# Squared-ReLU MLP on one core: block 0 opened with six whole-array f-tiles in place of four, worked off by row tiles of x, all first loads on one queue

## Chip, core and metric

One core of a Trainium2 chip (trn2). The metric is the device time of one execution in microseconds, median of the runs. One execution was also taken by the hardware profiler; all views of the profile and the trace are of that one.

## What is computed

Reference, cut to what matters (all tensors bf16):

```
B, S, D, F = 1, 2048, 576, 4608
h   = einsum("bsd,df->bsf", x, w1) + b1
r   = where(h > 0, h, 0)
out = einsum("bsf,fd->bsd", r * r, w2) + b2
```

That is two matrix products with a squared ReLU between them. x is 2048 x 576, w1 576 x 4608, w2 4608 x 576.

## The kernel before

**Tiling.** The 2048 rows of x are four blocks of 512 (`NSB`, `SB`), each of four row tiles of 128 (`RT`). The 4608 hidden features are 36 f-tiles of 128 (`NFT`). The contraction over D = 576 is four chunks of 128 (`NC`, the chunks 0 to 3) and a rest of 64 (rows 512 to 575).

**Phase A** computes the transposed, activated hidden values `hT` for every block: one PSUM bank of 128 x 512 floats for each f-tile. `a_step(b, j)` (L216) does two f-tiles at once, a *pair*: one of them uses rows 0 to 63 of the array and the other rows 64 to 127, in nine slices of 64 each (L213). This needs w1 in a form that holds 64 rows of D for one f-tile in the lower half of the partitions and 64 rows for the other in the upper half (`w1h`, loaded by `load_w1`, L97 to L99). `pairs` (L81) says which f-tiles make a pair; `slot` is its inverse. `evac_h` (L195) empties a bank: ACT does ReLU with the bias b1 (L197), DVE squares it (L199).

**Phase B** multiplies `hT` with w2 (L315, L329), adds b2 and stores.

**Block 0** is different at its start, since nothing has been loaded yet. Its first `G` = 4 f-tiles use the whole array, 128 rows deep: `qn` holds their four chunks of w1 (`load_quad`, L94), `qr` the rest of 64 rows (`load_rest`, L103). x arrives as it lies in memory, one row tile at a time (`load_x`, L91), is transposed on TensorE against an identity (L182) into PSUM, and copied from PSUM to `xT[0]` by DVE (L175) or ACT (L173). `transpose_chunks(half, cs, engs)` (L177) does this for *two* row tiles (a half, 256 columns) and the listed chunks; chunk `NC` stands for the last 128 columns of D and also fills the rest's place (L187). `full_mm(half, c)` (L225, L228) then multiplies chunk `c` of the four f-tiles with 256 columns of x. So this stage is two halves of 256 columns, and within each the four chunks. At its end four half-array matmuls add the rest (L254), three DVE copies put xT[0] into the form that the pair steps need (L256 to L258), and the four banks are emptied (L260). Then pair steps 2 to 17 follow (L292).

**What sets the order.** The schedule is written by hand: each engine works in the order of the program, and waits are for semaphores. The program order of L232 to L250 is TensorE's order. The eight first loads (four row tiles of x, four chunks of w1) are issued ahead of the start barrier (L126 to L140), alternating between SP's queue (x0, w1k0, w1k2, x3) and ACT's queue (x1, w1k1, x2, w1k3), where w1k0 is chunk 0 of w1 for the first f-tiles. Behind them SP issues the two rests and then the pairs of `w1h` in the order of their use (L121); a load takes one of eight semaphores in turn and waits until the load that used it before has landed. PSUM has eight banks; one takes the result of the five warm-up matmuls (L169), `G` of them are the f-tiles of block 0, and the remaining ones take transposes in turn. Blocks 1 to 3 read x by transposing DMAs (L266), behind the pair loads on SP. The pairs 0 and 1, which hold the first four f-tiles, are loaded after those of block 1 (L270) and come last in blocks 1 to 3 (L298).

Of the kernel before, what the change touches and what calls it, by code (L numbers as in the profile page):

```python
# [11 lines left out]
BF16 = mybir.dt.bfloat16  # L12
# [5 lines left out]
def kernel(  # L18
# [9 lines left out]
    nc = tc.nc  # L28
    P = 128
    H = 64  # L30
    x2 = x.flatten_outer_dims()
    out2 = out.flatten_outer_dims()
    S, D = x2.shape
    F = w1.shape[1]
    FH = F // 2
    G = 4
    NFT = F // P
    NJ = NFT // 2
    NC = D // P
    NH = D // H  # L40
    DM = NC * P
    SB = 512
    NSB = S // SB
    RT = SB // P
    HALF = SB // 2
# [9 lines left out]
    psum = ctx.enter_context(tc.tile_pool(name="psum", bufs=8, space=PSUM))  # L55

    def bank(name):
        return psum.tile([P, SB], FP32, name=name, tag="bank")
# [8 lines left out]
    at = [0]  # L67

    def early(n):
        at[0] += n  # L70
        assert at[0] <= NFT * D
        return w2_sb[:, at[0] - n:at[0]]


    xT = [early(XW).rearrange("p (w s) -> p w s", s=SB) for b in range(NSB - 1)]
    xT3 = xpool.tile([P, NH, SB], BF16, name="xT3", tag="xT3")
    xT.append(xT3[:])
    xs = early(RT * D).rearrange("p (j c) -> p j c", c=D)
    qn = early(NC * 4 * P).rearrange("p (c f) -> p c f", c=NC)
    qr = early(2 * P)  # L80
    pairs = [(0, 2), (1, 3)] + [(f, f + G) for f in range(G, NFT) if (f // G) % 2]  # L81
    slot = {ft: (h, j) for j, pr in enumerate(pairs) for h, ft in enumerate(pr)}
    assert len(pairs) == NJ and len(slot) == NFT

# [6 lines left out]
    def load_x(eng, j):  # L91
        eng.dma_start(out=xs[:, j, :], in_=x_view[:, j, :])

    def load_quad(eng, c):  # L94
        eng.dma_start(out=qn[:, c, :], in_=w1[c * P:(c + 1) * P, 0:G * P])

    def load_w1(eng, h, j0, n, cs):  # L97
        f0 = pairs[j0][h] * P
        eng.dma_start(out=w1h[h * H:(h + 1) * H, cs, j0 * P:(j0 + n) * P], in_=w1_rows[:, cs, f0:f0 + n * P])  # L99
# [1 line left out]
    NWARM = 5  # L101

    def load_rest(eng, h):  # L103
        eng.dma_start(out=qr[h * H:(h + 1) * H, :], in_=w1[DM:D, 2 * h * P:2 * (h + 1) * P])

    b1T = const.tile([P, NFT], FP32, name="b1T")
    warm = const.tile([P, 1], FP32, name="warm")
    load_x(nc.sync, 0)
    load_x(nc.scalar, 1)
    load_quad(nc.sync, 0)  # L110
    load_quad(nc.scalar, 1)
    load_quad(nc.sync, 2)
    load_x(nc.scalar, 2)
    load_x(nc.sync, 3)
    load_quad(nc.scalar, 3)
    nc.scalar.activation(out=warm[:], in_=nc.const_aps.tensor(1.0, [P, 1], FP32), func=ACT.Relu)
    for h in range(2):
        load_rest(nc.sync, h)


    for j0, n in ((2, 1), (3, 1), (4, 1), (5, 1), (6, 1), (7, 1), (8, 2), (10, 2), (12, 2), (14, 4)):  # L121
        for h in range(2):
            load_w1(nc.sync, h, j0, n, slice(0, NH))


    def issue_at_barrier(nc):  # L126
        entry, body = nc.main_func.blocks[:2]
        for engine in (mybir.EngineType.SP, mybir.EngineType.Activation):
            mine = [i for i in body.instructions if i.engine == engine and not isinstance(i, mybir.InstNoOp)]
            n = 0  # L130
            while isinstance(mine[n], mybir.InstDMACopy) and not mine[n].has_wait():
                n += 1
            assert n >= 3
            at = next(k for k, i in enumerate(entry.instructions)
                      if i.engine == engine and isinstance(i, mybir.InstEventSemaphore))
            for k, i in enumerate(mine[:n]):
                body.instructions.remove(i)
                entry.instructions.insert(at + k, i)

    nc.at_finalize(issue_at_barrier)  # L140


# [17 lines left out]
    ident = const.tile([P, P], BF16, name="ident")  # L160
# [10 lines left out]
    def copy_psum(eng, dst, src):  # L171
        if eng is nc.scalar:
            nc.scalar.copy(out=dst, in_=src)  # L173
        else:
            nc.vector.tensor_copy(out=dst, in_=src)  # L175

    def transpose_chunks(half, cs, engs):  # L177
        tps = [psum.tile([P, HALF], BF16, name="tp", tag="bank") for c in cs]
        for i in range(2):
            for c, tp in zip(cs, tps):  # L180
                d0 = c * P if c < NC else D - P
                nc.tensor.transpose(tp[:, i * P:(i + 1) * P], xs[:, 2 * half + i, d0:d0 + P], ident[:])  # L182
        cols = slice(half * HALF, (half + 1) * HALF)
        for c, tp, eng in zip(cs, tps, engs):
            copy_psum(eng, xT[0][:, c if c < NC else 7, cols], tp[:])
            if c == NC:
                nc.vector.tensor_copy(out=xT[0][0:H, 8, cols], in_=tp[H:P, :])  # L187

    def hT_of(b, ft):
        if b < NSB - 1:  # L190
            return hT[b][:, ft, :].rearrange("p (j s) -> p j s", j=RT)
        h, j = slot[ft]
        return w1h[:, h * RT:(h + 1) * RT, j * P:(j + 1) * P]

    def evac_h(b, ft, bk):  # L195
        r = rpool.tile([P, SB], BF16, name="r", tag="r")
        nc.scalar.activation(out=r[:], in_=bk[:], func=ACT.Relu, bias=b1T[:, ft:ft + 1], scale=1.0)  # L197
        r3 = r[:].rearrange("p (j s) -> p j s", j=RT)
        nc.vector.tensor_tensor(out=hT_of(b, ft), in0=r3, in1=r3, op=ALU.mult)  # L199

    def place(hi, c):
        if hi:
            return c // 2 if c % 2 else (3 + c // 2 if c else 8)
        return 8 if c == 8 else (4 if c % 2 else 0) + c // 2
# [11 lines left out]
    def a_step(b, j):  # L216
        bk = [bank("ph") for _ in range(2)]
        a_part(b, j, bk, range(NH))
        for h in range(2):
            evac_h(b, pairs[j][h], bk[h])  # L220


    bk0 = [bank("ph") for _ in range(G)]

    def full_mm(half, c):  # L225
        cols = slice(half * HALF, (half + 1) * HALF)
        for q in range(4):
            nc.tensor.matmul(bk0[q][:, cols], lhsT=qn[:, c, q * P:(q + 1) * P], rhs=xT[0][:, c, cols],  # L228
                             start=(half == 0 and c == 0), stop=False, skip_group_check=True)

    V, A = nc.vector, nc.scalar
    transpose_chunks(0, (0,), (V,))  # L232
    transpose_chunks(0, (1,), (A,))
    transpose_chunks(0, (2,), (A,))
    transpose_chunks(0, (NC,), (V,))
    full_mm(0, 0)
    transpose_chunks(0, (3,), (A,))
    full_mm(0, 1)
    full_mm(0, 2)
    transpose_chunks(1, (0, 1), (V, A))  # L240
    full_mm(0, 3)
    transpose_chunks(1, (2, NC), (A, V))
    full_mm(1, 0)
    transpose_chunks(1, (3,), (V,))
    full_mm(1, 1)
    b1T_ps = psum.tile([P, P], BF16, name="b1T_ps", tag="bank")
    nc.tensor.transpose(b1T_ps[:], b1_rows[:], ident[:])  # L247
    nc.vector.tensor_copy(out=b1T[:], in_=b1T_ps[:, 0:NFT])
    full_mm(1, 2)
    full_mm(1, 3)  # L250
    for i in range(2):
        for h in range(2):
            rows = slice(h * H, (h + 1) * H)
            nc.tensor.matmul(bk0[2 * h + i][:], lhsT=qr[rows, i * P:(i + 1) * P], rhs=xT[0][rows, place(h, 8), :],  # L254
                             start=False, stop=True, skip_group_check=True)
    nc.vector.tensor_copy(out=xT[0][0:H, 4:7, :], in_=xT[0][H:P, 0:3, :])  # L256
    nc.vector.tensor_copy(out=xT[0][H:P, 4:7, :], in_=xT[0][0:H, 1:4, :])
    nc.vector.tensor_copy(out=xT[0][H:P, 8, :], in_=xT[0][0:H, 0, :])  # L258
    for q in range(G):
        evac_h(0, q, bk0[q])  # L260


    def load_xT(b):
# [3 lines left out]

    load_xT(1)
    for h in range(2):
        load_w1(nc.sync, h, 0, 2, slice(0, NH))  # L270
    for b in range(2, NSB):
        load_xT(b)
    w2_view = w2_dram.rearrange("(ft p) d -> p ft d", p=P)
# [2 lines left out]
    def load_w2(c, n=1):  # L276
        nc.sync.dma_start(out=w2_sb[:, c * W2CH * D:(c + n) * W2CH * D].rearrange("p (ft d) -> p ft d", d=D),
                          in_=w2_view[:, c * W2CH:(c + n) * W2CH, :])
# [9 lines left out]
    def finish_xT(b):  # L288
        nc.vector.tensor_copy(out=xT[b][0:H, 8, :], in_=xT[b][H:P, 7, :])
        nc.vector.tensor_copy(out=xT[b][H:P, 8, :], in_=xT[b][0:H, 0, :])  # L290

    for j in range(2, NJ):  # L292
        a_step(0, j)
        if j == NJ - 2:
            finish_xT(1)
    load_w2(0)
    for b in range(1, NSB):
        for j in (*range(2, NJ), 0, 1):  # L298
            a_step(b, j)
            if j == NJ // 2 and b + 1 < NSB:  # L300
                finish_xT(b + 1)
        if b == 1:
            load_w2(1)
        if b == 2:
            load_w2(2, 2)
# [5 lines left out]
    for pr in range(NSB // 2):  # L311
        pc = bank("pc")
        for ft in range(NFT):
            for h in range(2):
                nc.tensor.matmul(pc[h * H:(h + 1) * H, :], lhsT=w2(ft, DM, D), rhs=hT_of(2 * pr + h, ft),  # L315
                                 start=(ft == 0), stop=(ft == NFT - 1))
# [52 lines left out]
```

## Time and profile before

| | us |
|---|---|
| median of 3 runs | 290.08 |
| lowest, highest | 289.96, 290.81 |
| the profiled execution | 290.45 |
| its span, first to last instruction | 288.7 |

The span is divided over TensorE's matmuls (PE, 99% busy), their weight loads (PEld, 46%), DVE (28%) and ACT (33%). Phase A lasts until about 145 us, phase B from there on. The stage that the change concerns is short: the first matmul of a pair step starts at 9.62 us.

How to read it: PE, DVE, ACT, POOL and SP are the engines TensorE, VectorE, ScalarE, GpSimd and SyncE. A line of the timeline gives start and length in us, the engine, the line of the kernel, the operation, what it writes and reads, how many, and in brackets how long the engine had been idle and for what. The buffers `xs`, `xT`, `qn` and `qr` are parts of `w2_sb`, since w2 comes later, so their names don't appear: "w_sb<-tp" is a copy from a transpose's bank into xT, "tp<-ident,w_sb" a transpose, "ph<-w_sb" a full_mm.

### The profile page before, as it was taken

The numbers are of one execution on the slowest core, as the hardware profiler recorded it, in microseconds if no ns is written. First come the engines' busy times: TensorE is split into PE (matmuls) and PEld (weight loads), VectorE is DVE, ScalarE is ACT, GpSimd is POOL, SyncE is SP. The second block draws the span as 40 slices with busy tenths as digits, with TensorE's granted clock in tenths as the row PEclk, the third lists the DMA queues.
The fourth block names the chain that finished last, engine by engine and source line by source line (L and its number), as shares of the span: only waits on it lengthen the run. The fifth ranks groups of instructions, "written<-read, shape, count | busy, mean of one in ns | idle before, by whom it ended". The sixth has DMA issues, their size and how long they took to land.

```text
span 288.7 us, 4818 instructions
## 1 busy us (share of the span) xinstructions
PE 284.9 (99%) x2067; PEld 133.7 (46%) x2078; DVE 79.5 (28%) x196; ACT 95.6 (33%) x153; POOL 1.5 (1%) x8
## 2 busy tenths in 40 slices
PE   9999999999999999999999999999999999999996
PEld 5544444444444444444445444444444444444454
DVE  1644454444445444444420011111100111111111
ACT  3666666766666676666620000000000000000000
POOL 2000000000000000000000000000000000000000
PEclk9999999999999999999999999999999999999999
DMA  7999999910400004300000100000000000000000
GB/s 200 205 190 204 172 185 208 321 50 2 122 3 0 3 2 142 106 0 2 0 2 19 20 20 20 20 23 5 15 20 23 20 20 20 23 20 22 20 23 20
DMA packets 35381, 18.01 MB, mean 62 GB/s; under 512 B 21652, under 2 KB 35360, under 8 KB 35360
## 3 DMA queue, kind: packets, MB, share of 16 engines
q1 hardware_dynamic: 34752, 17.14, 26.4%
q10 hardware_dynamic: 576, 0.56, 0.6%
q8 instruction: 16, 0.26, 0.4%
q14 instruction: 5, 0.04, 0.0%
q0 software_dynamic: 32, 0.01, 0.0%
HBM read 11.94 MB, written 2.36 MB: 50 GB/s over the span
## 4 chain that ended last, share of the span: by engine, by line
PE 98%; DMA 1%; issue 0%; DVE 0%; ACTq 0%
PE ph L213 47%; PE po L329 43%; PE pc L315 5%; PE ph L228 2%; DMA w_sb<-in_x_dram 1%; PE tp L182 1%; PE ph L254 0%; DVE o_sb L331 0%; PE b1T_ps L247 0%; ACTq L353 0%
## 5 line engine op out<-in xcount | busy, mean ns | idle before, releaser
L197 ACT ACTIVATE r<-ph,b1T 128x512 bf16<-128x512 f32 x144 | 91.0, 685 | 48.4 <-PE ph L213 46.4
L213 PE MATMUL ph<-w_sb,w1h 64*128 64x512 bf16 x936 | 101.2, 376 | 0.0
L213 PEld LDWEIGHTS <-w1h 64*128 64x128 bf16 x1260 | 61.3, 94 | 74.6
L329 PE MATMUL po<-w_sb,hT 128*128 128x512 bf16 x423 | 92.9, 379 | 0.5
L329 PEld LDWEIGHTS <-hT 128*128 128x128 bf16 x432 | 42.2, 98 | 51.2 <-issue 0.4
L199 DVE TENSOR_TENSOR hT<-r 128x512 bf16<-128x512 bf16 x108 | 46.0, 426 | 54.7 <-ACT r L197 54.2
L331 DVE TENSOR_TENSOR o_sb<-po,b_bc 128x512 bf16<-128x512 f32 (+2 forms) x17 | 11.2, 660 | 116.7 <-PE po L329 109.7
L213 PE MATMUL ph<-xT,w1h 64*128 64x512 bf16 x324 | 35.1, 376 | 0.0
L329 PE MATMUL po<-w_sb,w1h 128*128 128x512 bf16 (+2 forms) x178 | 31.2, 336 | 0.1
L329 PEld LDWEIGHTS <-w1h 128*128 128x128 bf16 x180 | 16.2, 98 | 15.3
L199 DVE TENSOR_TENSOR w1h<-r 128x512 bf16<-128x512 bf16 x36 | 15.3, 426 | 19.6 <-ACT r L197 19.5
L315 PE MATMUL pc<-hT,w_sb 128*64 128x512 bf16 x108 | 15.7, 379 | 0.0
L315 PEld LDWEIGHTS <-w_sb 128*64 128x64 bf16 x144 | 8.1, 110 | 7.6 <-issue 0.4
L315 PE MATMUL pc<-w1h,w_sb 128*64 128x512 bf16 x36 | 7.9, 379 | 0.0
L317 ACT ACTIVATE oc<-pc,b2T 128x512 bf16<-128x512 f32 x2 | 1.4, 687 | 13.7 <-PE pc L315 13.7
L325 DVE COPY o_sb<-oc 128x64 bf16<-128x64 bf16 x16 | 2.8, 172 | 9.3 <-DMA oc<-oc 9.3
L228 PE MATMUL ph<-w_sb 128*128 128x256 bf16 x32 | 5.3, 313 | 0.0
L228 PEld LDWEIGHTS <-w_sb 128*128 128x128 bf16 x32 | 3.4, 115 | 0.6
L175 DVE COPY w_sb<-tp 128x256 bf16<-128x256 bf16 x5 | 1.5, 292 | 5.9 <-PE tp L182 5.9
L182 PE MATMUL tp<-ident,w_sb 128*128 128x128 bf16 x20 | 2.7, 264 | 0.1
L169 PE MATMUL wps<-one 128*128 128x512 bf16 x5 | 2.3, 628 | 0.4 <-DVE one L144 0.4
L182 PEld LDWEIGHTS <-w_sb 128*128 128x128 bf16 x20 | 1.9, 118 | 1.4 <-DMA w_sb<-in_x_dram 1.2
(27 smaller groups left out, 10.7 us busy)
## 6 DMA issues: line engine op xcount, KB each, us to landing
w_sb<-in_w_dram SPq DMA_DIRECT2D x2, 1728.0 KB, 8.7
w1h<-in_w_dram SPq DMA_DIRECT2D x8, 288.0 KB, 5.9
out_dram<-o_sb SPq DMA_DIRECT2D x15, 144.0 KB, 1.8
w1h<-in_w_dram SPq DMA_DIRECT2D x12, 144.0 KB, 3.7
w_sb<-in_w_dram SPq DMA_DIRECT2D x2, 864.0 KB, 7.2
w1h<-in_w_dram SPq DMA_DIRECT2D x2, 576.0 KB, 11.2
w_sb<-in_x_dram SPq DMA_DIRECT2D x2, 144.0 KB, 3.4
w_sb<-in_x_dram ACTq DMA_DIRECT2D x2, 144.0 KB, 3.5
```

The source lines that it names most:

```text
L169: nc.tensor.matmul(wps[:], lhsT=ones[:, 0:P], rhs=ones[:], start=(i == 0), stop=(i == NWARM - 1))
L175: nc.vector.tensor_copy(out=dst, in_=src)
L182: nc.tensor.transpose(tp[:, i * P:(i + 1) * P], xs[:, 2 * half + i, d0:d0 + P], ident[:])
L197: nc.scalar.activation(out=r[:], in_=bk[:], func=ACT.Relu, bias=b1T[:, ft:ft + 1], scale=1.0)
L199: nc.vector.tensor_tensor(out=hT_of(b, ft), in0=r3, in1=r3, op=ALU.mult)
L213: nc.tensor.matmul(bk[h][:], lhsT=w1h[rows, c, j * P:(j + 1) * P], rhs=xT[b][rows, place(h, c), :], start=(i == 0), stop=(i == NH - 1))
L228: nc.tensor.matmul(bk0[q][:, cols], lhsT=qn[:, c, q * P:(q + 1) * P], rhs=xT[0][:, c, cols], start=(half == 0 and c == 0), stop=False, ski ...
L315: nc.tensor.matmul(pc[h * H:(h + 1) * H, :], lhsT=w2(ft, DM, D), rhs=hT_of(2 * pr + h, ft), start=(ft == 0), stop=(ft == NFT - 1))
L317: nc.scalar.activation(out=oc[:, pr, :], in_=pc[:], func=ACT.Identity, bias=b2T[:], scale=1.0)
L325: nc.vector.tensor_copy(out=o_sb[:, DM:D], in_=o_tr[pr][:, jj, h * H:(h + 1) * H])
L329: nc.tensor.matmul(po[:, 0:e - a], lhsT=hT_of(b, ft)[:, jj, :], rhs=w2(ft, a, e), start=(ft == 0), stop=(ft == NFT - 1))
L331: nc.vector.tensor_tensor(out=o_sb[:, a:e], in0=po[:, 0:e - a], in1=b2_bc[:, a:e], op=ALU.add)
```

## The change

Block 0 begins with six whole-array f-tiles in place of four (`G` = 6, `GP` = 3 pairs). The pairs are numbered anew: pairs 0 to 2 hold f-tiles 0 to 5, pairs 3 to 17 the others, and block 0 has the pair steps 3 to 17. The eight first loads are all issued on SP, in the order x0, w1k0, x1, w1k1, x2, w1k2, x3, w1k3, and w1's chunks are 768 columns wide instead of 512. ACT issues no loads any more. Transposes are made for each row tile by itself, two chunks into one bank (`transpose_tile`), with one copy of 2 x 128 columns by DVE or ACT; a third transpose holds the last 128 columns of D, with two copies. `full_mm(j, n, c)` multiplies chunk `c` of the six f-tiles with the columns of `n` row tiles from `j` on, so 128, 256 or 512 columns. The banks are emptied in the order of the rests. The late load of w1h has three pairs in place of two.

```diff
-    G = 4
+    G = 6
+    GP = G // 2
...
-    pairs = [(0, 2), (1, 3)] + [(f, f + G) for f in range(G, NFT) if (f // G) % 2]
+    pairs = [(i, GP + i) for i in range(GP)] + [(G + i, G + NJ - GP + i) for i in range(NJ - GP)]
...
-    load_x(nc.sync, 0)
-    load_x(nc.scalar, 1)
-    load_quad(nc.sync, 0)
-    load_quad(nc.scalar, 1)
-    load_quad(nc.sync, 2)
-    load_x(nc.scalar, 2)
-    load_x(nc.sync, 3)
-    load_quad(nc.scalar, 3)
+    for j in range(RT):
+        load_x(nc.sync, j)
+        load_quad(nc.sync, j)
...
-    for j0, n in ((2, 1), (3, 1), (4, 1), (5, 1), (6, 1), (7, 1), (8, 2), (10, 2), (12, 2), (14, 4)):
+    for j0, n in ((3, 1), (4, 1), (5, 1), (6, 1), (7, 1), (8, 1), (9, 1), (10, 2), (12, 2), (14, 4)):
...
+    def transpose_tile(j, c, n, eng):
+        cols = slice(j * P, (j + 1) * P)
+        tp = psum.tile([P, n, P], BF16, name="tp", tag="bank")
+        for k in range(n):
+            d0 = (c + k) * P if c < NC else D - P
+            nc.tensor.transpose(tp[:, k, :], xs[:, j, d0:d0 + P], ident[:])
+        c0 = c if c < NC else 7
+        copy_psum(eng, xT[0][:, c0:c0 + n, cols], tp[:])
+        if c == NC:
+            copy_psum(eng, xT[0][0:H, 8, cols], tp[H:P, 0, :])
...
+    V, A = nc.vector, nc.scalar
+    transpose_tile(0, 0, 2, V)
+    transpose_tile(0, 2, 2, A)
+    transpose_tile(0, NC, 1, V)
     bk0 = [bank("ph") for _ in range(G)]
...
+    def full_mm(j, n, c):
+        cols = slice(j * P, (j + n) * P)
+        for q in range(G):
             nc.tensor.matmul(bk0[q][:, cols], lhsT=qn[:, c, q * P:(q + 1) * P], rhs=xT[0][:, c, cols],
+                             start=(j == 0 and c == 0), stop=False, skip_group_check=True)
...
+    full_mm(0, 1, 0)
+    transpose_tile(1, 0, 2, V)
+    transpose_tile(1, 2, 2, A)
+    full_mm(1, 1, 0)
+    full_mm(0, 2, 1)
+    transpose_tile(1, NC, 1, V)
+    transpose_tile(2, 0, 2, A)
+    full_mm(2, 1, 0)
+    transpose_tile(2, 2, 2, V)
+    full_mm(2, 1, 1)
+    full_mm(0, 2, 2)
+    transpose_tile(2, NC, 1, A)
+    transpose_tile(3, 0, 2, V)
+    full_mm(3, 1, 0)
+    transpose_tile(3, 2, 2, A)
+    full_mm(3, 1, 1)
+    transpose_tile(3, NC, 1, V)
+    full_mm(2, 2, 2)
     b1T_ps = psum.tile([P, P], BF16, name="b1T_ps", tag="bank")
     nc.tensor.transpose(b1T_ps[:], b1_rows[:], ident[:])
     nc.vector.tensor_copy(out=b1T[:], in_=b1T_ps[:, 0:NFT])
+    full_mm(0, RT, 3)
```

The lines that these replace are in the kernel above (L177 to L187, L223 to L250).

More of the change, by code (lines that the diff above doesn't have):

```diff
@@ L78 @@
     xs = early(RT * D).rearrange("p (j c) -> p j c", c=D)
-    qn = early(NC * 4 * P).rearrange("p (c f) -> p c f", c=NC)
-    qr = early(2 * P)
-    pairs = [(0, 2), (1, 3)] + [(f, f + G) for f in range(G, NFT) if (f // G) % 2]
+    qn = early(NC * G * P).rearrange("p (c f) -> p c f", c=NC)
+    qr = early(GP * P)
+    pairs = [(i, GP + i) for i in range(GP)] + [(G + i, G + NJ - GP + i) for i in range(NJ - GP)]
     slot = {ft: (h, j) for j, pr in enumerate(pairs) for h, ft in enumerate(pr)}
@@ L103, in load_rest @@
     def load_rest(eng, h):
-        eng.dma_start(out=qr[h * H:(h + 1) * H, :], in_=w1[DM:D, 2 * h * P:2 * (h + 1) * P])
+        eng.dma_start(out=qr[h * H:(h + 1) * H, :], in_=w1[DM:D, GP * h * P:GP * (h + 1) * P])
     b1T = const.tile([P, NFT], FP32, name="b1T")
     warm = const.tile([P, 1], FP32, name="warm")
-    load_x(nc.sync, 0)
-    load_x(nc.scalar, 1)
-    load_quad(nc.sync, 0)
-    load_quad(nc.scalar, 1)
-    load_quad(nc.sync, 2)
-    load_x(nc.scalar, 2)
-    load_x(nc.sync, 3)
-    load_quad(nc.scalar, 3)
+    for j in range(RT):
+        load_x(nc.sync, j)
+        load_quad(nc.sync, j)
     nc.scalar.activation(out=warm[:], in_=nc.const_aps.tensor(1.0, [P, 1], FP32), func=ACT.Relu)
@@ L127, in issue_at_barrier @@
         entry, body = nc.main_func.blocks[:2]
[L128 to L138, printed above, removed]
+        engine = mybir.EngineType.SP
+        mine = [i for i in body.instructions if i.engine == engine and not isinstance(i, mybir.InstNoOp)]
+        n = 0
+        while isinstance(mine[n], mybir.InstDMACopy) and not mine[n].has_wait():
+            n += 1
+        assert n >= 2 * RT
+        at = next(k for k, i in enumerate(entry.instructions)
+                  if i.engine == engine and isinstance(i, mybir.InstEventSemaphore))
+        for k, i in enumerate(mine[:n]):
+            body.instructions.remove(i)
+            entry.instructions.insert(at + k, i)
     nc.at_finalize(issue_at_barrier)
@@ L175, in copy_psum @@
             nc.vector.tensor_copy(out=dst, in_=src)
[L177 to L187, printed above, removed]
+    def transpose_tile(j, c, n, eng):
[8 more added lines that the diff above has]
+            copy_psum(eng, xT[0][0:H, 8, cols], tp[H:P, 0, :])
     def hT_of(b, ft):
@@ L220, in a_step @@
             evac_h(b, pairs[j][h], bk[h])
+    V, A = nc.vector, nc.scalar
+    transpose_tile(0, 0, 2, V)
+    transpose_tile(0, 2, 2, A)
+    transpose_tile(0, NC, 1, V)
     bk0 = [bank("ph") for _ in range(G)]
-    def full_mm(half, c):
-        cols = slice(half * HALF, (half + 1) * HALF)
-        for q in range(4):
+    def full_mm(j, n, c):
+        cols = slice(j * P, (j + n) * P)
+        for q in range(G):
             nc.tensor.matmul(bk0[q][:, cols], lhsT=qn[:, c, q * P:(q + 1) * P], rhs=xT[0][:, c, cols],
[L229 to L245, printed above, removed]
+                             start=(j == 0 and c == 0), stop=False, skip_group_check=True)
[17 more added lines that the diff above has]
+    full_mm(2, 2, 2)
     b1T_ps = psum.tile([P, P], BF16, name="b1T_ps", tag="bank")
@@ L248 @@
     nc.vector.tensor_copy(out=b1T[:], in_=b1T_ps[:, 0:NFT])
-    full_mm(1, 2)
-    full_mm(1, 3)
-    for i in range(2):
+    full_mm(0, RT, 3)
+    for i in range(GP):
         for h in range(2):
             rows = slice(h * H, (h + 1) * H)
-            nc.tensor.matmul(bk0[2 * h + i][:], lhsT=qr[rows, i * P:(i + 1) * P], rhs=xT[0][rows, place(h, 8), :],
+            nc.tensor.matmul(bk0[GP * h + i][:], lhsT=qr[rows, i * P:(i + 1) * P], rhs=xT[0][rows, place(h, 8), :],
                              start=False, stop=True, skip_group_check=True)
@@ L258 @@
     nc.vector.tensor_copy(out=xT[0][H:P, 8, :], in_=xT[0][0:H, 0, :])
-    for q in range(G):
-        evac_h(0, q, bk0[q])
+    for i in range(GP):
+        for h in range(2):
+            evac_h(0, GP * h + i, bk0[GP * h + i])
     def load_xT(b):
@@ L269 @@
     for h in range(2):
-        load_w1(nc.sync, h, 0, 2, slice(0, NH))
+        load_w1(nc.sync, h, 0, GP, slice(0, NH))
     for b in range(2, NSB):
@@ L290, in finish_xT @@
         nc.vector.tensor_copy(out=xT[b][H:P, 8, :], in_=xT[b][0:H, 0, :])
-    for j in range(2, NJ):
+    for j in range(GP, NJ):
         a_step(0, j)
@@ L297 @@
     for b in range(1, NSB):
-        for j in (*range(2, NJ), 0, 1):
+        for j in (*range(GP, NJ), *range(GP)):
             a_step(b, j)
```

## The prediction

> **What bounds the kernel now.** I read the head of the page first, for whom the span belongs to.
>
> ```profile
> span 288.7 us, 4818 instructions
> PE 284.9 (99%) x2067; PEld 133.7 (46%) x2078; DVE 79.5 (28%) x196; ACT 95.6 (33%) x153; POOL 1.5 (1%) x8
> ```
>
> TensorE is busy for 99% of the span, so the change can gain only where TensorE idles or streams slowly, and loses wherever it makes TensorE wait. Next, the chain of work that ended last, in order of time (start, length, what). The change touches only its first 10 us.
>
> ```profile
> 0.21 2.84 DMA w_sb<-in_x_dram
> 3.04 0.05 issue
> 3.09 0.93 PE tp L182 x7
> 4.02 0.85 PE ph L228 x4
> 4.87 0.21 PE tp L182 x2
> 5.09 1.36 PE ph L228 x8
> 6.45 0.22 PE tp L182 x4
> 6.67 0.44 PE ph L228 x4
> ...
> 9.78 50.29 PE ph L213 x465
> ```
>
> See two things. After x1 lands at 3.05 no link but TensorE remains: no copy and no transfer of w1 is ever waited for. And the same four 128x256 matmuls take 0.85 us (0.213 each) at 4.02 and 0.44 (0.110) at 6.67; in thin slices of the timeline the starts go from 0.21 apart to 0.11 apart at 5.95 us. The array runs at half rate until 5.95. Four transposes take 0.22 us then, 0.055 for each 128 columns.
>
> Third, the timeline of all engines (start, length, engine, and in brackets the idle time before), for what a handoff costs.
>
> ```profile
> 3.42 0.29 DVE L175 COPY w_sb<-tp 128x256 bf16<-128x256 bf16 x1 [3.10 <-PE tp L182]
> ...
> 6.28 0.39 PE L182 MATMUL tp<-ident,w_sb 128*128 128x128 bf16 x4
> 6.65 0.29 DVE L175 COPY w_sb<-tp 128x256 bf16<-128x256 bf16 x1 [1.99 <-PE tp L182]
> 6.70 0.37 ACT L173 COPY w_sb<-tp 128x256 bf16<-128x256 bf16 x1 [1.21 <-PE tp L182]
> ...
> 9.17 0.11 PEld L254 LDWEIGHTS <-w_sb 64*128 64x128 bf16 x4 [0.21 <-issue]
> ...
> 9.62 35.56 PE L213 MATMUL ph<-w_sb,w1h 64*128 64x512 bf16 x328
> ```
>
> The transposes at 6.28 start 0.055 apart. The ACT copy at 6.70 begins 0.26 us after the last of them started (6.45) and takes 0.37; the DVE copy at 6.65 begins 0.26 after the third (6.39) and takes 0.29. So from the start of a transpose to a usable copy it is 0.63 us by ACT and 0.55 by DVE. Cold, the DVE copy at 3.42 began 0.33 after its transpose (3.09). In the kernel before, eight or more matmuls stand between, and nobody waits.
>
> Last, the busy time by stretches (us, then PE, PEld, DVE, ACT, POOL, clock, DMA share, GB/s): two queues early, and one queue of 1152-byte rows late.
>
> ```profile
> 2.00:2.50 0.50, 0.50 (x2) 0.00 (x0) 0.00 (x0) 0.35 (x1) 0.42 (x1) 1.00 1.07 375
> ...
> 54.00:55.00 1.00, 1.00 (x14) 0.45 (x10) 0.27 (x1) 0.51 (x1) 0.00 (x0) 1.00 1.09 386
> ```
>
> One queue moves as much as two (386 against 375 GB/s).
>
> **What the Trainium skill says.** "TensorE: Matmul & The Clock Gate", section "What's actually happening": the array's clock is halved until one free-running window of about 3.4 us was busy. The trace agrees on the halving (0.213 against 0.110 us) and puts the release at 5.95; which share of a window must be busy it doesn't show. The same page, "Step-by-step: what each phase is for": weight loads may be pulled ahead, matmuls stay in program order; so one matmul that waits for a copy stops all behind it. Section "Back-to-back issue gap": a stream of load and matmul pairs with 128 columns is sustained at some 81 ns each; this trace shows 55 in bursts of four. "DMA: Bandwidth & Descriptors", section "Issuing engines are not separate DMA queues": all queues share the 16 engines, a second issuer saves only issue time; the two rates above agree.
>
> **The change part by part.** The two kernels are compared where six f-tiles of block 0 are streamed; from there on both run the same pair steps.
>
> Streaming: before, four f-tiles of 4x512 columns, 2x512 for the paired rests, and one pair step of 9x512: 13,824 columns. After, 6x4x512 + 3x512 = 13,824. Both have 20 transposes of x and one of b1. So nothing is saved in streaming. Before reaches this point at 9.62 + 1.94 (a pair step: 35.56/328 x 18 = 1.95; copies of successive pairs come 1.94 apart) = 11.56 us. Cutting 128x512 into 128 and 256 columns adds some 2.5 ns a matmul (0.110 against 0.107): under 0.1 us.
>
> Transfers: eight on SP, 0.44 us of issue each (SP's row for L92, L95: 0.39 to 0.43), so the last is issued at 3.6 instead of 2.0. In order they hold 147, 344, 492, 688, 836, 1032, 1180, 1376 KB in sum. Before, x0 landed at 2.69 and the first four transfers (557 KB) by 3.7. With the same ramp I put x0, w1k0, x1, w1k1, x2, w1k2, x3, w1k3 at 2.7, 3.2, 3.7, 4.2, 4.7, 5.4, 5.8, 6.4. TensorE asks for them, by the working below, at 2.7, 3.5, 4.3, 5.6, 6.5, 8.0, 8.7, 11.0. Even at 200 GB/s (the mean of 18 to 30 us) from 1.1 us on, and 0.4 for the landing, all but x0 would be there in time (w1k1, 688 KB: 4.9; w1k3, 1376 KB: 8.4); none costs anything. The rests and the pair loads queued behind on SP start at 4.9 instead of 4.3, but the first pair is wanted at 13, not at 9.6, and a pair (295 KB at 200 GB/s: 1.5 us) is used up in 1.94: cover 3 us or more. ACT loses four issues, and its table load (at 2.15 now) may come sooner; its first copy is not waited for.
>
> Start: TensorE needs x0 only, and no longer idles until x1 (2.82 to 3.09 less the fill, 0.25 us at half rate): a gain of 0.13 in full-rate time.
>
> New waits, in program order, with 0.05 us from the copy's end to the matmul (the trace shows no such wait; the other way round, PE to DVE or ACT, takes 0.03 to 0.04, so between 0.02 and 0.10):
> 1. Three groups of transposes, 2.71 to 3.24 (five at 0.107). The first copy: second transpose's start 2.82 + 0.33 + 0.29 + 0.05 = 3.49. TensorE waits 0.25 at half rate. Then six matmuls to 4.15.
> 2. Row tile 1: four transposes from 4.15 to 4.58; its first copy is ready at 4.26 + 0.33 + 0.29 + 0.05 = 4.93: wait 0.35, at half rate. Six matmuls to 5.6, and w1k1 (six of 256 columns, the clock rising in them) to 6.4.
> 3. Row tile 2: its copy is on ACT and full_mm(2,1,0) comes right after the transposes, with nothing between: 0.63 + 0.05 - 0.055 = 0.63 us, at full rate.
> 4. Row tile 3, on DVE, likewise: 0.55 + 0.05 - 0.055 = 0.55.
> 5. full_mm(2,2,2) needs the ACT copy of row tile 3, behind six matmuls and one transpose (0.39): 0.63 + 0.05 - 0.39 - 0.03 = 0.26.
> Full-rate waits: 0.63 + 0.55 + 0.26 = 1.44. The half-rate ones, 0.60, count half as long as the release stays at 5.95 (work not streamed before it is streamed after it in half the time): 0.30. Sum: 1.44 + 0.30 - 0.13 = +1.6 us. Walking the same working through the kernel before gives its first pair step at 9.42 against the 9.62 recorded; the 0.2 is the "issue" before the half-array weights, which both have.
>
> After that point: six banks are copied out by ACT (0.69 each) instead of four; two banks are free for the next step, and the third step needs two of the six 1.9 us after the first is done, when ACT has finished them (1.4). No wait. The copies of L256 to L258 (1.39 us on DVE) end before the step's sixth slice asks. x of block 1 landed at 36.5 and is wanted at 40.7. The rest is untouched.
>
> So +1.6 us on the profiled execution (290.45, its span 288.7 and 1.75 outside): 292.1. That one stood 0.37 above the median of the runs, so the forecast is 290.08 + 1.6 = 291.7.
>
> Bounds: handoffs -0.1 to +0.2; 128-column matmuls at 81 ns instead of 55, 24 of them warm: 0 to +0.6; x0 landing sooner without x1 beside it: -0.1 to 0; the release between 4 and 7 us: -0.7 to +0.5. Together 291.0 to 292.5.
>
> **The rivals.**
> Late clock. Waits 1 and 2 take 0.60 of the 3.4 us before 5.95, so that window is 82% busy, where it was 93%. If that isn't enough, the release comes a window later, at 9.36: 3.4 us more run at half rate (1.7 lost), and wait 3 then counts half (0.3 back): 1.6 + 1.7 - 0.3 = +3.0, so 293.1. For it: the window of the warm-up matmuls, some 63% busy, was not enough. Against: 82 is nearer to 93.
>
> Early clock, no slower. The window runs free. If the release falls at 2.5 to 3.0 us, right behind the warm-up matmuls, which now run into the transposes without the gap at 2.7, the 3.2 us from 2.71 to 5.95 stream at full rate (1.6 gained), and waits 1 and 2 count in full, some 0.85 with the quicker groups before them: 1.44 + 0.85 - 0.13 - 1.6 = +0.55, so 290.6, within 0.3%. A release before about 3.5 us is the point from which it decides. Against it: the trace of before shows 5.95 with the same warm-up.
>
> Transfers bind after all. If one queue brings the eight 1.06 us apart, twice the 0.53 of my times, w1k0 lands at 3.8, x1 at 4.8, w1k1 at 5.9, x2 at 6.9 and w1k3 at 10.1: TensorE then waits at half rate for w1k0 (0.5, in place of wait 1), x1 (0.4) and the copy behind it (0.4), and later for x2 (0.1): 0.65 + 0.1 + 1.44 - 0.13 = +2.1, so 292.2. The 386 GB/s on one queue speak against it.
>
> **How the numbers follow.** The forecast's case has 0.58, binding transfers 0.05, late clock 0.16, early clock 0.15, a gain for a reason that I don't see 0.06. 0.3% is 0.87 us, about what a measurement of this kernel can tell from no change: faster 0.06, same 0.15, slower 0.79. The range runs from the early clock with handoffs 0.1 shorter (290.5) to the late clock with handoffs 0.2 longer (293.3), which leaves out little more than the unseen gain.
>
> **What would show it.** In the profile after, waits of the full matmuls for DVE and ACT copies of about 0.3, 0.4, 0.6, 0.55 and 0.25 us before 11 us; none for a transfer but x0; the first pair step at about 13.2; the page from there as before. Wrong would be: a pair step by 12, matmuls waiting for w1, 128-column matmuls 80 ns apart, or 0.21 us for 256 columns still after 6.5.

## The result and the profile after

| | before, us | after, us |
|---|---|---|
| median (lowest to highest) | 290.02 (289.95 to 290.81), 4 runs | 292.02 (291.50 to 292.22), 4 runs |
| profiled execution | 290.45 | 291.50 |
| its span | 288.7 | 289.7 |
| first matmul of a pair step in it | 9.62 (step 2) | 12.62 (step 3) |

The ratio of after to before, of the means, is 1.0060, with a 95% interval of 1.0038 to 1.0082. The forecast was 291.7, from +1.6 us; the medians lie 2.0 us apart.

The head of the page after, to be held against the one of before:

```profile
span 289.7 us, 4844 instructions
PE 284.8 (98%) x2078; PEld 134.1 (46%) x2090; DVE 79.8 (28%) x199; ACT 95.5 (33%) x154; POOL 1.5 (1%) x8
```

TensorE's busy time, as the profile counts it, is the same to 0.1 us; the span is 1.0 us longer. What was added is idle time. The chain that ended last shows where, in order of time (start, length, what):

```profile
0.53 2.80 DMA w_sb<-in_w_dram
3.33 0.05 issue
3.38 0.82 PE ph L227 x6
4.20 0.23 PE tp L178 x2
4.43 0.02 issue
4.45 0.30 DVE w_sb L171
4.75 0.04 issue
4.79 1.24 PE ph L227 x12
6.03 0.18 PE tp L178 x3
6.21 0.02 issue
6.24 0.38 ACT w_sb L169
6.62 0.04 issue
...
8.46 0.30 DVE w_sb L171
8.76 0.04 issue
...
9.45 0.38 ACT w_sb L169
9.83 0.04 issue
```

Before, this chain stayed on TensorE from 3.09 us on. Now it leaves TensorE four times for a copy, DVE, ACT, DVE, ACT in turn, and once at the start for w1k0. Each time the pattern is the same: transposes, 0.02 us, a copy, 0.04 us, matmuls. The timeline gives the lengths:

```profile
3.99 0.63 PE L178 MATMUL tp<-ident,w_sb 128*128 128x128 bf16 x4
...
4.79 1.24 PE L227 MATMUL ph<-w_sb 128*128 128x128 bf16 x12 [0.17 <-DVE w_sb L171]
...
5.87 0.33 PE L178 MATMUL tp<-ident,w_sb 128*128 128x128 bf16 x3
...
6.66 0.49 PE L227 MATMUL ph<-w_sb 128*128 128x128 bf16 x6 [0.46 <-ACT w_sb L169]
...
8.09 0.33 PE L178 MATMUL tp<-ident,w_sb 128*128 128x128 bf16 x3
...
8.80 0.49 PE L227 MATMUL ph<-w_sb 128*128 128x128 bf16 x6 [0.38 <-DVE w_sb L171]
...
9.58 0.22 PE L178 MATMUL tp<-ident,w_sb 128*128 128x128 bf16 x1
...
9.87 0.81 PE L227 MATMUL ph<-w_sb 128*128 128x256 bf16 x6
```

The brackets show less than what is lost. They count from the end of the last transpose's record, which is 0.22 us long (0.31 at half rate), while transposes that follow closely start every 0.055 us (0.107 at half rate). Counted from the start of the last transpose plus that step, TensorE waits 0.37 us before 4.79, 0.62 before 6.66, 0.54 before 8.80 and 0.23 before 9.87: the last transposes start at 4.31, 5.98, 8.20 and 9.58.

One quantity ties all runs together. The time of the profiled execution minus the start of its first pair step is 290.45 - 9.62 = 280.83 us before and 291.50 - 12.62 = 278.88 after, 1.95 apart, which is the pair step that six f-tiles save. After that point both kernels take the same time. So all of the difference, 12.62 - (9.62 + 1.94) = 1.06 us in this pair of executions, lies ahead of the first pair step.

The forecast's +1.6 stood for two releases of the clock at the same moment. They were not: the trace's record of the granted full clock begins at 5.95 us before and at 4.50 after. By the forecast's own rule (half of the time that TensorE streams, so from 4.79 to 5.95) that is worth some 0.6 us. With the release at 5.95 the changed kernel would have had its first pair step at about 13.2 us, as forecast, and the difference would have been some 1.6 us; both are estimates.

### The profile page after: what moved, and what is told of

Read it like the earlier page. It is cut to its first block, busy times and chain, and to the rows that moved or that the text cites. A ratio compares the mean times of both kernels' runs of the same rounds, so it can differ in the third digit from the quotient of the medians.

```text
span 289.7 us, 4844 instructions
## 1 busy us (share of the span) xinstructions
PE 284.8 (98%) x2078; PEld 134.1 (46%) x2090; DVE 79.8 (28%) x199; ACT 95.5 (33%) x154; POOL 1.5 (1%) x8
## 4 chain that ended last, share of the span: by engine, by line
PE 97%; DMA 1%; issue 0%; DVE 0%; ACT 0%; SPq 0%
PE ph L208 46%; PE po L331 43%; PE pc L317 5%; PE ph L227 2%; DMA w_sb<-in_w_dram 1%; PE tp L178 0%; ACT w_sb L169 0%; PE ph L255 0%; DVE w_sb L171 0%; SPq L93 0%; DVE o_sb L333 0%; PE b1T_ps L249 0%; SPq L355 0%
## 5 line engine op out<-in xcount | busy, mean ns | idle before, releaser
L208 PE MATMUL ph<-w_sb,w1h 64*128 64x512 bf16 x918 | 99.2, 376 | 0.0
L208 PEld LDWEIGHTS <-w1h 64*128 64x128 bf16 x1242 | 60.4, 94 | 73.6
L227 PE MATMUL ph<-w_sb 128*128 128x128 bf16 (+2 forms) x59 | 6.7, 258 | 1.3 <-DVE w_sb L171 0.6
L227 PEld LDWEIGHTS <-w_sb 128*128 128x128 bf16 x60 | 4.7, 102 | 2.7 <-issue 1.6
L171 DVE COPY w_sb<-tp 128x256 bf16<-128x256 bf16 (+2 forms) x10 | 2.5, 251 | 7.5 <-PE tp L178 7.4
L169 ACT COPY w_sb<-tp 128x256 bf16<-128x256 bf16 (+2 forms) x6 | 2.0, 336 | 5.6 <-PE tp L178 5.6
```

Of the source, the lines that this page charges most:

```text
L208: nc.tensor.matmul(bk[h][:], lhsT=w1h[rows, c, j * P:(j + 1) * P], rhs=xT[b][rows, place(h, c), :], start=(i == 0), stop=(i == NH - 1))
```

## The experiments

The theory: TensorE, in program order, waits for copies that come right behind their transposes. The rivals: the single queue and its later transfers; six f-tiles as such; the release of the clock. For each run, "step" is the start of the first pair step in its profile.

**Covered order.** Only TensorE's work in block 0 is altered: its order, and two groups of 256 columns are split into four of 128, so that their halves can stand apart:

```diff
     full_mm(1, 1, 0)
-    full_mm(0, 2, 1)
-    transpose_tile(1, NC, 1, V)
+    full_mm(0, 1, 1)
     transpose_tile(2, 0, 2, A)
+    full_mm(1, 1, 1)
+    transpose_tile(1, NC, 1, V)
     full_mm(2, 1, 0)
     transpose_tile(2, 2, 2, V)
     full_mm(2, 1, 1)
-    full_mm(0, 2, 2)
     transpose_tile(2, NC, 1, A)
     transpose_tile(3, 0, 2, V)
-    full_mm(3, 1, 0)
+    full_mm(0, 2, 2)
+    full_mm(2, 1, 2)
     transpose_tile(3, 2, 2, A)
+    full_mm(3, 1, 0)
     full_mm(3, 1, 1)
     transpose_tile(3, NC, 1, V)
-    full_mm(2, 2, 2)
+    full_mm(3, 1, 2)
```

> The changed kernel with nothing but the order of TensorE's work in block 0 altered, so that matmuls on older row tiles stand between a transpose and the first matmul that reads its copy. Waiting for copies (the theory): the waits of 0.62, 0.5 and 0.2 us in row tiles 2 and 3 go, about 0.2 stays before row tile 2; 1.1 us faster than the changed kernel, so some 0.6 us above the kernel before. One queue, or six f-tiles as such: no change, +1.7 to +2.0 us. Clock release: it follows no order of the program, so runs spread as before by some 0.8 us, and the profile's first pair step moves by half of what its release moves.

Measured: 290.87 us median of 8 runs against 290.03, ratio 1.0028 (1.0017 to 1.0038). The step came at 11.83 us, 0.79 before the changed kernel's, though its clock was released at 5.07, 0.57 later. The changed kernel streamed for 0.28 us of these 0.57 (from 4.79 on); half of that added, the order alone is worth some 0.9 us, where 1.1 was expected. It does not take back the whole loss: the run stands 0.84 us above the kernel before. The timeline shows what is left:

```profile
3.88 0.63 PE L178 MATMUL tp<-ident,w_sb 128*128 128x128 bf16 x4
4.68 1.04 PE L227 MATMUL ph<-w_sb 128*128 128x128 bf16 x12 [0.17 <-DVE w_sb L171]
5.72 0.28 PE L178 MATMUL tp<-ident,w_sb 128*128 128x128 bf16 x2
...
6.18 0.22 PE L178 MATMUL tp<-ident,w_sb 128*128 128x128 bf16 x1
6.46 0.49 PE L227 MATMUL ph<-w_sb 128*128 128x128 bf16 x6
```

The wait before 4.68 was left in it, and one of 0.22 us before 6.46 too (6.46 - 6.18 - 0.055). The transposes at 5.72 now wait some 0.2 us for x2, which landed at 5.67.

**Two queues.** The changed kernel with w1's chunks on ACT's queue:

```diff
     for j in range(RT):
         load_x(nc.sync, j)
-        load_quad(nc.sync, j)
+        load_quad(nc.scalar, j)
```

> The changed kernel with the four loads of w1's chunks on ACT's queue, x staying on SP's. Waiting for copies: x0 lands some 0.4 us later because w1k0 runs beside it, w1k0 sooner; within 0.3 us of the changed kernel, so +1.5 to +2.0 us on the kernel before. One queue as the cause: back to within 0.5 us of the kernel before.

Measured: 291.33 us against 290.03, 1.0050 (1.0038 to 1.0062). Its interval overlaps the changed kernel's, and its profile has the same waits (6.41 for ACT, 8.55 for DVE). Two queues alone bring no gain that the runs can tell; the queue by itself is not where the time went.

**Four f-tiles.** The changed kernel with `G = 4` (and the pair loads of before, from pair 2 on):

> The changed kernel's order and single queue, but four whole-array f-tiles as before. Waiting for copies: the waits stay, four matmuls instead of six hide 0.1 us less before the last; +1.6 to +2.1 us on the kernel before. Six f-tiles (their matmuls of 128 columns, their larger loads) as the cause: back to within 0.5 us of the kernel before.

Measured: 291.40 us against 290.03, 1.0050 (1.0038 to 1.0062). The loss stays with four f-tiles. In its profile TensorE waits for ACT and DVE copies in the same places, and here the last wait is long enough to have a bracket too:

```profile
PE ph L227 <- ACT w_sb L169: 0.6, 2, 0.5
PE ph L227 <- DVE w_sb L171: 0.6, 2, 0.4
```

A line gives the engine and line that waited, for whom, us in total, times, longest. The brackets hold 1.2 us, for four waits.

**The kernel before, exposed.** Two queues and four f-tiles as before; only the order around the second half is altered, so that its matmuls come right behind their transposes:

```diff
-    transpose_chunks(1, (0, 1), (V, A))
     full_mm(0, 3)
-    transpose_chunks(1, (2, NC), (A, V))
+    transpose_chunks(1, (0, 1), (V, A))
     full_mm(1, 0)
-    transpose_chunks(1, (3,), (V,))
     full_mm(1, 1)
+    transpose_chunks(1, (2, NC), (A, V))
+    transpose_chunks(1, (3,), (V,))
```

> The kernel before, two queues and four f-tiles, with the matmuls of the second half moved so that they come right behind the transposes that they need. Waiting for copies: about 0.5 us for chunk 0, 0.1 for chunk 1, 0.45 for chunk 2 and 0.1 for the last, all at full rate: +1.1 us on the kernel before, with neither one queue nor six f-tiles. One queue or six f-tiles as the cause: no change.

Measured: 291.44 us against 290.03, 1.0049 (1.0037 to 1.0061), +1.4. The loss of the change can be made in the old kernel without any other part of the change. The size is not clean, though:

```profile
PE ph L228 <- DMA w_sb<-in_w_dram: 0.6, 1, 0.6
...
PE ph L228 <- DVE w_sb L175: 0.3, 1, 0.3
PE ph L228 <- ACT w_sb L173: 0.2, 1, 0.2
```

Moving full_mm(0, 3) ahead of four transposes made it wait 0.6 us for w1k3, which nobody had waited for. The two copies' waits, with the 0.17 us each that the brackets leave out (0.22 - 0.055), come to some 0.9.

**Covered order on two queues.** As the covered order, with w1 on ACT's queue, with w1k1's first matmuls behind the second row tile's transposes, and with half of chunk 3's matmuls moved up between the transposes of the last row tile. The order against that of the covered run, in part:

```diff
     transpose_tile(1, 2, 2, A)
-    full_mm(1, 1, 0)
     full_mm(0, 1, 1)
+    full_mm(1, 1, 0)
     transpose_tile(2, 0, 2, A)
     full_mm(1, 1, 1)
     transpose_tile(1, NC, 1, V)
+    full_mm(0, 2, 2)
     full_mm(2, 1, 0)
     transpose_tile(2, 2, 2, V)
     full_mm(2, 1, 1)
     transpose_tile(2, NC, 1, A)
     transpose_tile(3, 0, 2, V)
-    full_mm(0, 2, 2)
+    full_mm(0, 2, 3)
...
-    full_mm(0, RT, 3)
+    full_mm(2, 2, 3)
```

> Six f-tiles with the covered order of the run before and the loads of w1 on ACT's queue, so that w1k1 and x2 land sooner and the first matmuls of w1k1 can stand behind the second row tile's transposes. Waiting for copies: nothing but the first copy (0.25 at half rate) is left; +0.0 to +0.5 us on the kernel before. Six f-tiles as the cause of what the covered order left (0.8): still +0.8.

Measured: 290.37 us against 290.41, 0.9999 (0.9991 to 1.0007). All six f-tiles, all matmuls of 128 columns, the larger loads and the row-tile order of x are in it, and it is as fast as the kernel before, within some 0.3 us. So none of these costs more than that by itself. The order alone left 0.84 us, two queues alone left 1.3, and both together leave nothing that can be measured. How much of the 0.84 the second queue took back, and how much the further changes of order, no run separates.

**The kernel before on one queue.** Its eight first loads all on SP, in the same order (`nc.scalar` replaced by `nc.sync` in L109 to L115):

> The kernel before with its eight first loads on SP's queue in the same order x0 x1 w1k0 w1k1 w1k2 x2 x3 w1k3. Waiting for copies: nothing of the 1.7 us comes from the queue itself, x1 lands some 0.3 us later (at half rate 0.15) and w1k3 is needed at 6.5 and lands about then; 0.0 to +0.4 us. One queue as the cause: +0.8 us or more.

Measured: 290.88 us against 290.41, 1.0019 (1.0011 to 1.0026): +0.5, a little above what was expected. One queue is not free here, for a reason that the expectation didn't name (engine and line, for whom, us in total, times, longest):

```profile
PE tp L182 <- DMA w_sb<-in_x_dram: 0.8, 2, 0.6
PE ph L213 <- DMA w1h<-in_w_dram: 0.5, 1, 0.5
```

There x2 and x3, which stand sixth and seventh on one queue, come late for the second half; and SP, busy with issues until 3.8, starts the pair loads at 5.17 instead of 4.30, so that at 22.4 us a pair step waits for its w1. The changed kernel's pair loads start at 5.17 too, but its first pair step is 3 us later.

**Repeats.** Both kernels again, for the release of the clock:

> The changed kernel unaltered, beside the others on the same chip. Waiting for copies: +1.7 to +2.0 us on the kernel before. If the moment of the clock's release is the same in every run, its profile shows 4.50 us again; if it runs free, another, with the first pair step later or earlier than 12.62 by about half of the difference.

> The kernel before unaltered, for its profile alone. If the release runs free of the program, it falls elsewhere than at 5.95 us, the first pair step moves from 9.62 by about half of the difference (not below 9.1, where its copies begin to be waited for), and the time of the execution moves with it, by the same amount; if not, all three repeat.

The changed kernel: 291.62 us against 290.41, 1.0041 (1.0027 to 1.0054). Its profiled execution took 293.58. In the trace's record the clock was released at 9.64 us, the first pair step was at 14.69, and the rest took 293.58 - 14.69 = 278.89 us, as in the first pair of profiles. Five microseconds of later release cost 2.07. Half rate shows directly:

```profile
1.00 3.23 DMA w_sb<-in_x_dram
...
5.05 2.08 PE L227 MATMUL ph<-w_sb 128*128 128x128 bf16 x12 [0.17 <-DVE w_sb L171]
```

The same twelve matmuls took 1.24 us in the profile after. The first line is the load of x1 in the chain that ended last: it landed at 4.23, and TensorE stood still for it from 3.89 to 4.28. So in this execution a transfer was waited for, besides the copies. The kernel before: 290.23, step at 9.39. This trace has no record of its clock's release, but the transposes after 4.5 us start 0.057 apart, so it lay at about 4.4: 1.5 us earlier than in the first profile, for a gain of only 0.23. From there on it waits for transfers, which half rate had hidden: for w1k2, which landed at 5.3, and for x3, at 6.0. The two profiles whose releases lie closest, 4.50 after and about 4.4 before, put the cost of the change at 12.62 - 9.39 - 1.94 = 1.29 us.

**Four f-tiles covered**, and the six beside it, for a version that might beat both kernels. The former is the covered version on two queues with `G = 4`; the latter is that version unaltered.

> The covered order on two queues with four whole-array f-tiles instead of six, so that the first loads are 262 KB smaller and land sooner; a try for a version that beats both. Waiting for copies: like the covered version with six, -0.3 to +0.1 us on the kernel before (the start on x0 alone gains 0.1, shorter cover may cost as much). Six f-tiles as a cause of loss: clearly below the covered version with six, -0.5 us or more.

> The covered version with six f-tiles on two queues, beside the one with four on the same chip: within 0.3 us of the kernel before, as in its first run. Its profile shows another release of the clock than 3.42 us if that runs free.

Measured: four 290.37 us against 290.25, 1.0000 (0.9991 to 1.0009); six 290.30, 1.0007 (0.9996 to 1.0018). Neither beats the kernel before, and four against six makes no difference that can be measured. In six's profile the release came at 3.81 us, in the first profile of that kernel at 3.42.

## Why the prediction was right, point by point

The time, 291.7 against 292.02, and the sign were right, and so was the cause in the main: with the copies covered and two queues the loss goes, with two queues alone it stays, and in the exposed kernel, with neither one queue nor six f-tiles, a loss of this kind comes. That the forecast lies within 0.3 us is in part luck: by the medians the change cost 2.0 us in the first set of runs and 1.2 in the repeat.

*Streaming saves nothing.* Right: six f-tiles covered equal four covered and the kernel before. The matmuls of 128 columns start 0.055 us apart in the profile after (six in 0.49 us, of which 0.16 is the way through the array), so the 81 ns of the Trainium skill ("TensorE: Matmul & The Clock Gate", section "Back-to-back issue gap") don't hold here, for groups of six to twelve.

*The waits.* Predicted 0.25, 0.35, 0.63, 0.55, 0.26; measured, counted as above, 0.36, 0.37, 0.62, 0.54, 0.23. The handoff from a copy to the matmul was taken at 0.05 and is 0.04. The first wait was not for the copy, which was ready at 3.24, but for w1k0, which landed at 3.33.

*Transfers.* This step failed in size. Times of 2.7, 3.2, 3.7, 4.2, 4.7, 5.4, 5.8 and 6.4 were given; they landed at 2.3, 3.3, 3.8, 5.2, 5.6, 6.4, 6.9 and 7.5 (issue and time to landing of each). "One queue moves as much as two" was read from a stretch at 54 us with 1152-byte rows; at the start it didn't hold. The same stretch before and after (GB/s at the end of the line):

```profile
1.00:5.00 4.00, 3.89 (x19) 2.07 (x18) 0.88 (x3) 2.12 (x4) 1.10 (x3) 1.00 0.95 282
...
1.00:5.00 4.00, 3.68 (x23) 2.17 (x22) 1.03 (x4) 1.93 (x4) 1.10 (x3) 1.00 0.89 242
```

The forecast's times stand for 1229 KB from x0's landing to the last one in 3.7 us, 332 GB/s; the measured ones for the same bytes in 5.2 us, 236 GB/s. Whether a second queue saves only the time to issue, as the prediction has it, is not settled by this: the eighth load was issued at 3.37 us instead of 1.58, and no run tells this from the queue itself. "None costs anything" was nearly true all the same in this profile, because TensorE, waiting for copies, asked late: 0.1 us for w1k0, and under 0.1 for w1k1, which landed at 5.16. In the repeat x1 cost 0.39 us at half rate. In the first covered version, where TensorE asks sooner, x2 cost some 0.2 us, and in the two-queue one still 0.3 in its second profile.

*The start on x0 alone.* Right in kind, larger: x0 landed at 2.3 us, and the first transpose started at 2.49 instead of 2.71.

*The range.* The bounds given, 291.0 to 292.5, are narrower than their own terms added up (290.8 to 293.0), which the prediction doesn't explain; 292.02 lies in both.

*The clock.* The rule (work not streamed at half rate takes half the time later) held: 2.07 us for 5.14 us of release in the changed kernel, where half of a wait that falls into the slow time is given back. The step that it gave, about 13.2, was for a release at 5.95. What failed is the reference: "the trace of before shows 5.95 with the same warm-up" was taken as typical. Over the ten profiles that record it the release lay between 3.4 and 9.6 us, in no order with the edits. So a single pair of executions can differ by about a microsecond for this alone, and 1.06 in the profiles and 2.0 between the medians don't contradict each other. The size of the loss from the two sets of runs is 1.2 to 2.0 us.

*The rivals.* Late clock did happen, in 1 of 10 executions of the changed kernel (293.58; worked out as 293.1), and a run of 292.64 of a covered version may be another; it isn't the usual case. Its reading of the trace was off: it took the window before 5.95 as 93% busy, which allows for the idle time before x1 (2.82 to 3.09) and leaves out that before x0 (2.53 to 2.71). By the starts of the matmuls, transposes counted, that window was busy for 87%. The section "What's actually happening" of the Trainium skill's page "TensorE: Matmul & The Clock Gate" has windows of about 3.4 us. Counted back from each release, in all ten profiles, the windows that led to a release were busy for 79% (covered on two queues, release 3.42) to 87% (before, and the first profile after). The window from 2.82 to 6.23 in the late execution was busy for about 70% (idle from 3.02 to 3.29 and from 4.68 to 5.05 for copies, from 3.89 to 4.28 for x1) and led to none. So waits in the first microseconds can go with a lost window, and the wait for a transfer was here as long as the longest one for a copy; that the waits were the cause, and how often it happens, was not tried. Early clock was not met: the changed kernel's own profiles show releases at 4.50 and 9.64 us, and one before 3.5 us, the forecast's point of decision, was seen only in the covered version. The nearest is the changed kernel on two queues, released at 3.73, in 291.25 us. Transfers that bind: refuted as a main cause by the two-queue run, though not as a part of the loss, since one queue cost the kernel before 0.5 us.

## What to carry to other kernels

On an engine that works in program order, the time from a transpose's start to the use of its copy (0.60 us by DVE, 0.68 by ACT here) has to be filled with work whose operands are already there; cutting the work into finer tiles shortened that filling here, so the order must be reworked with the tile size. When a covered order is moved forward, the next thing that it meets is a transfer: check each operand's landing against the new time of use, as the exposed kernel's 0.6 us shows. And compare short stages by a mark inside the program, here the first pair step, since behind it all runs of the same number of f-tiles agreed to 0.04 us, but for the one on one queue that waited later.

## What the runs showed of the hardware that was not expected

- The release of TensorE's clock fell at 3.42, 3.65, 3.73, 3.81, 3.84, 4.50, 4.68, 5.07, 5.95 and 9.64 us in the profiles that record it, twice differently for the same kernel (4.50 and 9.64; 3.42 and 3.81). The full clock is recorded for 283.31 or 286.72 us in every one of them, 3.41 apart, which fits windows of that length.
- At the start of the program, from 1 to 5 us, the five profiles with the first loads on one queue show 218 to 251 GB/s, the seven with two queues 277 to 314; at 54 us a single queue moved 386. The length of w1's rows isn't the reason: with rows of 1024 bytes it was 218 and 246 on one queue against 277 to 283 on two, with rows of 1536 bytes 242 to 251 against 302 to 314. Whether the later issue, at some 0.47 us from one load to the next, or the queue itself is the reason, the runs don't tell.
- Matmuls with weight loads of their own started 0.055 us apart for 128 columns and 0.109 for 256, in groups of up to twelve, at full rate.
